# Moving 64 output columns of a second matmul from row-wise tiles of 512 to a transposed, full-array tile of 128

## The chip, the cores and the metric

The kernel runs on one core of a Trainium2 chip. The metric is device time in microseconds (us). The profile's "span", from the first to the last instruction of the program, is about 1.8 us shorter than the time that is quoted.

Two ways of reading matmul records are used below. The profile's lines give the busy time of groups of instructions. Where a line is not fine enough I use the *step*: the time from the start of one matmul record to the start of the next on TensorE. Matmuls overlap in the pipeline (a 512-column one is recorded as 379 ns, but one starts every 216 ns), so it is the steps, not the durations, that add up to the span. Steps are computed from start times in the traces.

## The reference

```python
# x: [1, 2048, 576], w1: [576, 4608], w2: [4608, 576], all bf16
h = x @ w1 + b1
h = relu(h) ** 2
out = h @ w2 + b2          # [1, 2048, 576]
```

## The kernel before

Rows are handled in four blocks of 512 (`SB`). The first matmul leaves `hT`, the hidden values transposed: 36 tiles (`NFT`) of 128 hidden features x 512 rows per block. Its contraction length, 576, is four and a half times 128. For 32 of the 36 tiles all of it is done in nine steps of 64 with *row tiles*: pairs of matmuls on 64 of the array's rows each, which run side by side. For the other four tiles (of three blocks; the first block does it in smaller pieces) four steps of 128 use the full array, and only the remaining half a step is a row tile.

The second matmul has 576 output columns and two forms. The first 512 are computed row-wise: 128 rows of `hT` are the stationary operand, 512 columns of `w2` stream past. The last 64 are computed transposed: 64 columns of `w2` are stationary, 512 rows of `hT` stream. As 64 columns fill half of the array, two blocks are done side by side as two column tiles, each with its own half of the partitions of PSUM, the memory that matmuls write to. That needs both blocks' `hT`, so the phase comes once per two blocks, and its result is transposed back by a DMA.

In the cuts below, `keep` holds an instruction in program order; `...` marks what is left out.

```python
SB = 512; DM = 512; DT = D - DM          # DT = 64
EDGES = [0, 384, 512]                    # the last tile alone is cut in two

def phase_t(sb):                         # blocks sb and sb + 1 together
    pt = ps_o.tile([P, SB], FP32, name="pt", tag="po")
    for i, ft in enumerate(t_order):
        for h in range(2):
            keep(nc.tensor.matmul(pt[h * DT:(h + 1) * DT, :], lhsT=w2_sb[:, ft, DM:D], rhs=hTs[sb + h][:, ft, :],
                                  start=(i == 0), stop=(i == NFT - 1)))
    # ... + bias on ScalarE, DMA transpose, one output DMA per block

def phase_b(sb, hT, last=False, dups=()):
    for jj in range(RT):                 # 4 tiles of 128 rows
        # ...
        edges = EDGES if last and jj == RT - 1 else [0, DM]
        for d0, d1 in zip(edges, edges[1:]):
            po = ps_o.tile([P, 512], FP32, name="po", tag="po")
            for i, ft in enumerate(ft_order):
                keep(nc.tensor.matmul(po[:, 0:d1 - d0], lhsT=hT[:, ft, jj * P:(jj + 1) * P],
                                      rhs=w2_sb[:, ft, d0:d1], start=(i == 0), stop=(i == NFT - 1)))
            # ... + bias on VectorE into o_sb, output DMA on the sync queue

# order on TensorE, once for blocks 0 and 1, once for blocks 2 and 3 (the two "halves"):
a_rows(1); a_full(1, "rows_first")       # row tiles, then full array
phase_t(0)                               # column tiles
phase_b(0, hTs[0], dups=(2, 3)); phase_b(1, hTs[1])     # full array
```

Of the kernel before, what the change touches and what calls it, by code (L numbers as in the profile page):

```python
# [17 lines left out]
def kernel(  # L18
# [9 lines left out]
    nc = tc.nc  # L28
    keep = tc.keep_in_program_order
    P = 128  # L30
    H = 64
    x2 = x.flatten_outer_dims()
    out2 = out.flatten_outer_dims()
    S, D = x2.shape
    F = w1.shape[1]
    NFT = F // P
# [6 lines left out]
    assert D == 576 and S % 512 == 0 and F % (2 * P) == 0  # L43
    SB = 512
    RT = SB // P
    DM = 512
    DT = D - DM

    const = ctx.enter_context(tc.tile_pool(name="const", bufs=1))
    wpool = ctx.enter_context(tc.tile_pool(name="wpool", bufs=1))  # L50
# [46 lines left out]
    nc.gpsimd.memset(b1_rows[:], 0.0)  # L97
    nc.gpsimd.dma_start(out=b1_rows[0:NFT, :], in_=b1.rearrange("(ft p) -> ft p", p=P))
    b2_col = const.tile([P, 1], BF16, name="b2_col")
    for h in range(2):  # L100
        nc.gpsimd.dma_start(out=b2_col[h * DT:(h + 1) * DT, :], in_=b2[DM:D].rearrange("(d o) -> d o", o=1))
    b2T = const.tile([P, 1], FP32, name="b2T")
    nc.gpsimd.tensor_copy(out=b2T[:], in_=b2_col[:])
    warm = const.tile([P, 1], FP32, name="warm")
# [25 lines left out]
    w2_sb = wpool.tile([P, NFT, D], BF16, name="w2_sb")  # L130
# [39 lines left out]
    hTs = {}  # L170
# [92 lines left out]
        ft_order += [G + j, G + NJ + j]  # L263

    t_order = ft_order[G:] + ft_order[:G]
    EDGES = [0, 384, 512]

    def phase_t(sb):
        pt = ps_o.tile([P, SB], FP32, name="pt", tag="po")
        for i, ft in enumerate(t_order):  # L270
            for h in range(2):
                keep(nc.tensor.matmul(pt[h * DT:(h + 1) * DT, :], lhsT=w2_sb[:, ft, DM:D], rhs=hTs[sb + h][:, ft, :],  # L272
                                      start=(i == 0), stop=(i == NFT - 1)))
        oT = tpool.tile([P, SB], BF16, name="oT", tag="oT")
        keep(nc.scalar.activation(out=oT[:], in_=pt[:], func=ACT.Identity, bias=b2T[:], scale=1.0))  # L275
        ot = tpool.tile([P, RT, P], BF16, name="ot", tag="ot")
        keep(nc.sync.dma_start_transpose(out=ot[:, :, :], in_=oT[:, :]))
        for h in range(2):
            r0 = (sb + h) * SB
            dst = out2[r0:r0 + SB, DM:D].rearrange("(j p) d -> p j d", p=P)  # L280
            keep(nc.sync.dma_start(out=dst, in_=ot[:, :, h * DT:(h + 1) * DT]))

    def phase_b(sb, hT, last=False, dups=()):
        for jj in range(RT):
            if jj < len(dups):
                dup_windows(dups[jj])
            rt = sb * RT + jj
            o_sb = opool.tile([P, DM], BF16, name="o_sb", tag="o_sb")
# [6 lines that stand above are left out]
                keep(nc.vector.tensor_tensor(out=o_sb[:, d0:d1], in0=po[:, 0:d1 - d0], in1=b2_bc[:, d0:d1], op=ALU.add))  # L295
                keep(nc.sync.dma_start(out=out2[rt * P:(rt + 1) * P, d0:d1], in_=o_sb[:, d0:d1]))
# [20 lines left out]
    load_xT(3)  # L317
    a_rows(1)
    a_full(1, "rows_first")
    phase_t(0)  # L320
    phase_b(0, hTs[0], dups=(2, 3))
    phase_b(1, hTs[1])
    alloc_hT(2)
# [2 lines left out]
    alloc_hT(3)  # L326
    a_rows(3)
    a_full(3, "rows_first")
    phase_t(2)
    phase_b(2, hTs[2])  # L330
    phase_b(3, hTs[3], last=True)

# [29 lines left out]
```

## Time and profile before

| | before |
|---|---|
| time, median of 3 runs (lowest to highest) | 291.75 us (291.16 to 291.76) |
| span of the profiled run | 289.8 us |
| TensorE busy | 98% |
| second matmul, row-wise (L293) | 123.8 us busy |
| second matmul, transposed (L272) | 15.9 us busy |

These are lines of the profile page of the kernel before: busy time and share of the span per engine, the clock per fortieth of the span, and the chain of work that ended last.

```profile
span 289.8 us, 4679 instructions
PE 285.1 (98%) x2017; PEld 133.7 (46%) x2032; DVE 79.5 (27%) x176; ACT 95.2 (33%) x152; POOL 2.8 (1%) x11
PEclk9999999999999999999999999999999999999999
PE 98%; issue 0%; DVE 0%
```

TensorE (PE) is busy 98% of the time and is 98% of the chain; no other engine is over 33% (PEld is TensorE's own weight loads, which overlap its matmuls). A change here is worth what it changes on TensorE.

### The profile page before, as it was taken

Reading aid. Unit: us, or ns where it says so; the run is one execution under the profiler, and the core shown is the slowest. Engines: PE = TensorE matmul, PEld = TensorE weight load, DVE = VectorE, ACT = ScalarE, POOL = GpSimd, SP = SyncE. Lnnn points to the kernel's source line nnn. Section 1 sums busy time; section 2 is a strip of 40 time slices with the busy share of each in tenths; the row PEclk is TensorE's granted clock in tenths of the full one; section 3 lists DMA queues with packets and bytes.
Section 4 is the critical chain, followed back from the end, with each engine's and each line's share of the span. In section 5 each row is a group of like instructions: output and inputs, shape, how many; then the busy total and the mean of one; then the engine's idle time right before and its main releaser. Section 6 shows DMA issues by size and latency. Waiting matters only on the chain.

```text
span 289.8 us, 4679 instructions
## 1 busy us (share of the span) xinstructions
PE 285.1 (98%) x2017; PEld 133.7 (46%) x2032; DVE 79.5 (27%) x176; ACT 95.2 (33%) x152; POOL 2.8 (1%) x11
## 2 busy tenths in 40 slices
PE   8999999999999999999999999999999999999996
PEld 5544444444444444444444444444445444444454
DVE  1644554444502100000025444444440000000001
ACT  2666666666500000000027666666670000000000
POOL 3000000000000000000000000000000000000000
PEclk9999999999999999999999999999999999999999
DMA  7999999400001000000000000000000200000000
GB/s 198 213 235 185 315 388 234 83 0 2 0 19 33 5 20 18 18 18 20 18 18 2 1 2 0 2 0 2 0 2 0 38 18 18 18 20 18 20 18 20
DMA packets 30581, 16.26 MB, mean 56 GB/s; under 512 B 14676, under 2 KB 30560, under 8 KB 30560
## 3 DMA queue, kind: packets, MB, share of 16 engines
q1 hardware_dynamic: 30176, 15.65, 21.7%
q8 instruction: 16, 0.26, 0.4%
q10 hardware_dynamic: 288, 0.30, 0.4%
q14 instruction: 5, 0.04, 0.0%
q0 software_dynamic: 96, 0.01, 0.0%
HBM read 11.36 MB, written 2.36 MB: 47 GB/s over the span
## 4 chain that ended last, share of the span: by engine, by line
PE 98%; issue 0%; DVE 0%
PE po L293 43%; PE ph L189 42%; PE pt L272 5%; PE pn L210 4%; PE pn L228 1%; PE wps L63 1%; PE tb L150 1%; PE ph L191 1%; PE pn L204 1%; DVE o_sb L295 0%; PE b1T_ps L167 0%; PE pn L206 0%
## 5 line engine op out<-in xcount | busy, mean ns | idle before, releaser
L191 PE MATMUL ph<-xTw,w_h 64*128 64x512 bf16 x576 | 124.6, 376 | 0.0
L189 PE MATMUL ph<-xTw,w_h 64*128 64x512 bf16 x576 | 124.6, 376 | 0.0
L293 PE MATMUL po<-w_sb,hT 128*128 128x512 bf16 (+2 forms) x600 | 123.8, 366 | 0.8 <-issue 0.3
L177 ACT ACTIVATE r<-ph,b1T 128x512 bf16<-128x512 f32 x128 | 81.0, 684 | 41.7 <-PE ph L191 41.7
L293 PEld LDWEIGHTS <-hT 128*128 128x128 bf16 x612 | 58.3, 98 | 66.7 <-issue 0.8
L189 PEld LDWEIGHTS <-w_h 64*128 64x128 bf16 x576 | 54.1, 94 | 68.3
L178 DVE TENSOR_TENSOR hT<-r 128x512 bf16<-128x512 bf16 x144 | 61.1, 425 | 75.9 <-ACT r L177 75.4
L191 PEld LDWEIGHTS <-w_h 64*128 64x128 bf16 x576 | 54.1, 94 | 0.0
L295 DVE TENSOR_TENSOR o_sb<-po,b_bc 128x512 bf16<-128x512 f32 (+2 forms) x17 | 11.2, 660 | 125.0 <-PE po L293 125.0
L177 ACT ACTIVATE r<-pn,b1T 128x512 bf16<-128x512 f32 x16 | 10.3, 687 | 68.7 <-PE pn L206 67.4
L272 PE MATMUL pt<-hT,w_sb 128*64 128x512 bf16 x144 | 15.9, 380 | 0.0
L272 PEld LDWEIGHTS <-w_sb 128*64 128x64 bf16 x144 | 8.0, 110 | 7.8 <-issue 0.8
L210 PE MATMUL pn<-xTw,w1n 128*128 128x512 bf16 x45 | 10.4, 379 | 0.4 <-issue 0.3
L210 PEld LDWEIGHTS <-w1n 128*128 128x128 bf16 x48 | 4.5, 98 | 6.0 <-issue 0.8
L275 ACT ACTIVATE oT<-pt,b2T 128x512 bf16<-128x512 f32 x2 | 1.4, 687 | 14.5 <-PE pt L272 14.5
L228 PE MATMUL pn<-xTw,w1n 128*128 128x256 bf16 x32 | 4.8, 304 | 0.0
L228 PEld LDWEIGHTS <-w1n 128*128 128x128 bf16 x32 | 3.4, 110 | 0.6
L63 PE MATMUL wps<-const-bfloat16-1.0 128*128 128x512 bf16 (+1 forms) x7 | 2.8, 581 | 0.8 <-PEq L346 0.8
L157 DVE COPY xTw<-tb 128x256 bf16<-128x256 bf16 x4 | 1.1, 292 | 6.6 <-PE tb L150 6.6
L120 DVE COPY xTw<-xTw 64x2048 bf16<-64x2048 bf16 x4 | 2.8, 690 | 0.2
L121 DVE COPY xTw<-xTw 64x2048 bf16<-64x2048 bf16 x4 | 2.7, 687 | 0.1
L159 ACT COPY xTw<-tb 128x256 bf16<-128x256 bf16 x4 | 1.3, 375 | 3.7 <-PE tb L150 3.7
(23 smaller groups left out, 16.9 us busy)
## 6 DMA issues: line engine op xcount, KB each, us to landing
w_sb<-in_w_dram SPq DMA_DIRECT2D x6, 864.0 KB, 9.6
w_h<-in_w_dram SPq DMA_DIRECT2D x14, 288.0 KB, 6.8
out_dram<-o_sb SPq DMA_DIRECT2D x15, 128.0 KB, 1.7
w_h<-in_w_dram SPq DMA_DIRECT2D x4, 144.0 KB, 3.6
w1n<-in_w_dram SPq DMA_DIRECT2D x4, 128.0 KB, 3.7
x_sb<-in_x_dram ACTq DMA_DIRECT2D x2, 144.0 KB, 2.8
x_sb<-in_x_dram SPq DMA_DIRECT2D x2, 144.0 KB, 3.3
out_dram<-ot SPq DMA_DIRECT2D x4, 64.0 KB, 1.8
```

The lines of the kernel that those rows point to most:

```text
L63: keep(nc.tensor.matmul(wps[:, 0:n], lhsT=ones[:, 0:P], rhs=ones[:, 0:n], start=True, stop=True))
L150: keep(nc.tensor.transpose(bank[:, slot, qc], xs[:, j, c0:c0 + P], ident[:]))
L177: keep(nc.scalar.activation(out=r[:], in_=bank[:], func=ACT.Relu, bias=b1T[:, ft:ft + 1], scale=1.0))
L178: keep(nc.vector.tensor_tensor(out=hTs[sb][:, ft, :], in0=r[:], in1=r[:], op=ALU.mult))
L189: keep(nc.tensor.matmul(bx[:], lhsT=w1_h[0:H, LO_C[i], jc], rhs=xT[0:H, LO_W[i], :], start=(i == 0), stop=(i == NC - 1)))
L191: keep(nc.tensor.matmul(by[:], lhsT=w1_h[H:P, UP_C[i], jc], rhs=xT[H:P, UP_W[i], :], start=(i == 0), stop=(i == NC - 1)))
L204: keep(nc.tensor.matmul(banks[2 * i][:], lhsT=w1n8[0:H, i, :], rhs=xT[0:H, SPC, :], start=start, stop=stop, skip_group_check=order == "k_o ...
L210: keep(nc.tensor.matmul(banks[g][:], lhsT=w1n[:, k, g * P:(g + 1) * P], rhs=xT[:, O + k, :], start=start, stop=stop))
L228: keep(nc.tensor.matmul(banks[g][:, hc], lhsT=w1n[:, k, g * P:(g + 1) * P], rhs=xT[:, O + k, hc], start=(h == 0 and k == 0), stop=False, s ...
L272: keep(nc.tensor.matmul(pt[h * DT:(h + 1) * DT, :], lhsT=w2_sb[:, ft, DM:D], rhs=hTs[sb + h][:, ft, :], start=(i == 0), stop=(i == NFT - 1)))
L293: keep(nc.tensor.matmul(po[:, 0:d1 - d0], lhsT=hT[:, ft, jj * P:(jj + 1) * P], rhs=w2_sb[:, ft, d0:d1], start=(i == 0), stop=(i == NFT - 1)))
L295: keep(nc.vector.tensor_tensor(out=o_sb[:, d0:d1], in0=po[:, 0:d1 - d0], in1=b2_bc[:, d0:d1], op=ALU.add))
```

## The change

The transposed part takes 128 columns instead of 64. Then it fills the array by itself, needs no column tiles and no second block, and runs once per block. The row-wise part shrinks from 512 to 448 columns.

```diff
-    DM = 512
-    DT = D - DM
+    DT = P
+    DM = D - DT
 ...
-    for h in range(2):
-        nc.gpsimd.dma_start(out=b2_col[h * DT:(h + 1) * DT, :], in_=b2[DM:D].rearrange("(d o) -> d o", o=1))
+    nc.gpsimd.dma_start(out=b2_col[:], in_=b2[DM:D].rearrange("(d o) -> d o", o=1))
 ...
-    EDGES = [0, 384, 512]
+    EDGES = [0, 320, DM]
 
-    def phase_t(sb):
+    def phase_t(sb, hT):
         pt = ps_o.tile([P, SB], FP32, name="pt", tag="po")
         for i, ft in enumerate(t_order):
-            for h in range(2):
-                keep(nc.tensor.matmul(pt[h * DT:(h + 1) * DT, :], lhsT=w2_sb[:, ft, DM:D], rhs=hTs[sb + h][:, ft, :],
-                                      start=(i == 0), stop=(i == NFT - 1)))
+            keep(nc.tensor.matmul(pt[:], lhsT=w2_sb[:, ft, DM:D], rhs=hT[:, ft, :],
+                                  start=(i == 0), stop=(i == NFT - 1)))
 ...                                     # one output DMA per call instead of two
-    phase_t(0)
+    phase_t(0, hTs[0])
+    phase_t(1, hTs[1])
 ...
-    phase_t(2)
+    phase_t(2, hTs[2])
+    phase_t(3, hTs[3])
```

More of the change, by code (lines that the diff above doesn't have):

```diff
@@ L277, in phase_t @@
         keep(nc.sync.dma_start_transpose(out=ot[:, :, :], in_=oT[:, :]))
-        for h in range(2):
-            r0 = (sb + h) * SB
-            dst = out2[r0:r0 + SB, DM:D].rearrange("(j p) d -> p j d", p=P)
-            keep(nc.sync.dma_start(out=dst, in_=ot[:, :, h * DT:(h + 1) * DT]))
+        dst = out2[sb * SB:(sb + 1) * SB, DM:D].rearrange("(j p) d -> p j d", p=P)
+        keep(nc.sync.dma_start(out=dst, in_=ot[:, :, :]))
     def phase_b(sb, hT, last=False, dups=()):
```

## The prediction

> **What bounds the kernel now.** TensorE, almost alone. The page's busy line gives PE 285.1 of 289.8 us (98%), DVE 27%, ACT 33%; the chain of waits is 98% PE, "issue" 0%; the granted clock is 1.000. Matmuls overlap in the pipeline, so I cost them by start-to-start steps between consecutive PE records. At 512 columns a full-array matmul starts every 216 ns; at 384 every 162.5 ns; at 128 every 56 ns. They lie on columns / 2.4 + about 2.6 ns, which is what the Trainium skill ("TensorE: Matmul & The Clock Gate", "Back-to-back issue gap") gives for the isolated gap, N/2.4 + 2.5. The weight loads (about 98 ns each in the groups by line) hide even under 56 ns steps. A pair of 64-column tiles (two matmuls 3 to 4 ns apart) also takes 216 ns per pair.
>
> **What is removed, added, moved.**
> Removed: 64 columns of each row-wise matmul. 540 of them go from 512 to 448 columns (estimate 448/2.4 + 2.6 = 189.3 ns): 540 x 26.7 ns = 14.4 us. The split last tile goes from 384 to 320: 36 x 26.7 = 1.0 us. Together -15.38 us.
> Added: the transposed part goes from 72 pairs of column tiles at 216 ns (15.55 us) to 144 full-array matmuls at 216 ns (31.1 us): +15.55 us. In columns streamed the two cancel exactly (576 x 64 = 72 x 512); what stays, +0.17 us, is the fixed 2.6 ns of 72 more slots.
> Also removed: the changes of array mode. The Trainium skill ("TensorEngine Tiling (Array Packing)", "Key Properties") says that a change of tiling mode drains the array. This trace agrees: entering the column-tile phase the step is 309 ns in place of 216 (+93), its first pair's step is 237 (+21), and leaving it the step is 537 (+321). That is 0.44 us for each of two phases, 0.87 us, and all of it goes, as the phase now has the mode of its neighbours. The row-tile changes (steps of 535 ns) stay.
> Off the path: two more ACT evictions of 0.69 us, two more output transposes, 448 in place of 512 columns on DVE (0.69 us each, every 7.8 us). Every po tile is drained long before its bank is needed again. The tail (last 128 columns, one 0.29 us eviction, one output DMA) stays as it is.
>
> **On the critical path:** all PE terms. 15.55 - 15.38 - 0.87 = -0.7 us, 0.25%.
>
> **Predicted time:** 291.0 us; 8 in 10 between 290.2 and 291.7. Faster by over 2%: 0.01; within 2%: 0.98; slower by over 2%: 0.01.
>
> **What would show it.** Row-wise matmuls of 128x448 at steps of 189 ns; transposed ones at 216 ns, 144 of them, both phases together 31.1 us against 16.4 us; no step above 220 ns on entering or leaving the transposed phases; row-wise output 109 us against 124; PE still 98% of the chain; granted clock still 1.000.
>
> **What would make it wrong.** 448-column steps longer than 189 ns (weight loads no longer hidden, or a floor); the drain remaining for another reason than the mode, which makes it +0.15 us slower in place of 0.7 faster; a lower clock from denser use of the array; a bank wait from two transposed accumulators in a row. Only steps of 200 ns or more at 448 columns would cost 2%.

## More of the kernel before

The groups by line and shape, of the kernel before; the columns are line, engine, operation, output<-inputs, array rows*columns, partitions x elements, count, then busy us and mean ns of one, then idle time before them.

```profile
L293 PE MATMUL po<-w_sb,hT 128*128 128x512 bf16 x528 | 115.9, 379 | 0.8 <-issue 0.3
L272 PE MATMUL pt<-hT,w_sb 128*64 128x512 bf16 x144 | 15.9, 380 | 0.0
L210 PE MATMUL pn<-xTw,w1n 128*128 128x512 bf16 x45 | 10.4, 379 | 0.4 <-issue 0.3
```

The 144 matmuls of L272 are 72 pairs; "128*64" is the column tile. On the profile page 2017 matmuls were recorded, but 2032 weight loads; each matmul has one weight load, so 15 matmul records are missing: L293 should have 540 of this shape and has 528, L210 should have 48 and has 45. The idle time "issue" in the last column belongs to those gaps.

The timeline of TensorE at the first transposed phase, kernel before (start us, length us, engine, line, operation, count, idle time before):

```profile
73.13 3.40 PE L210 MATMUL pn<-xTw,w1n 128*128 128x512 bf16 x15 [0.16 <-issue]
76.46 7.96 PE L272 MATMUL pt<-hT,w_sb 128*64 128x512 bf16 x72
84.58 1.67 PE L293 MATMUL po<-w_sb,hT 128*128 128x512 bf16 x7 [0.16 <-issue]
```

The phase of column tiles starts at 76.46 and the next one at 84.58 us, 8.12 us for 36 pairs, where 36 x 216 ns would be 7.78. The program has 16 matmuls of L210 here; 15 are in the trace. The matmul that is missing is the first one, which is why the line is marked with idle time.

Last, what the sync queue waited for at the end of the program (line 357 stands for the closing instructions; columns: in total us, times, longest):

```profile
SPq L357 <- DMA out_dram<-o_sb: 0.7, 1, 0.7
```

## The result and the profile after

| | before | changed |
|---|---|---|
| median (lowest to highest) | 291.47 us (291.16 to 291.76), 4 runs | 291.15 us (291.01 to 291.35), 4 runs |
| ratio, 95% interval | | 0.9992 (0.9978 to 1.0006) |
| five more rounds: median | 291.46 us, 9 runs | 291.18 us, 5 runs |
| ratio, 95% interval | | 0.9991 (0.9978 to 1.0003) |

A ratio and its interval are from runs of the same rounds; a ratio is not quite that of the medians (291.15 / 291.47 = 0.9989). Both intervals include 1: by the clock of whole runs the two kernels are the same.

The same lines of the changed kernel: page (with the chain last), groups, timeline, and the sync queue's wait.

```profile
span 289.4 us, 4699 instructions
PE 285.2 (99%) x2032; PEld 138.9 (48%) x2032; DVE 78.5 (27%) x176; ACT 96.7 (33%) x154; POOL 2.3 (1%) x10
PEclk9999999999999999999999999999999999999999
PE 97%; DMA 1%; SPq 0%; DVE 0%; issue 0%
```

```profile
L289 PE MATMUL po<-w_sb,hT 128*128 128x448 bf16 x540 | 102.5, 352 | 0.0
L270 PE MATMUL pt<-hT,w_sb 128*128 128x512 bf16 x144 | 31.4, 379 | 0.0
L209 PE MATMUL pn<-xTw,w1n 128*128 128x512 bf16 x48 | 10.9, 379 | 0.0
```

```profile
72.46 3.63 PE L209 MATMUL pn<-xTw,w1n 128*128 128x512 bf16 x16
75.92 15.70 PE L270 MATMUL pt<-hT,w_sb 128*128 128x512 bf16 x72
91.46 1.87 PE L289 MATMUL po<-w_sb,hT 128*128 128x448 bf16 x9
```

```profile
SPq L355 <- DMA out_dram<-o_sb: 1.1, 1, 1.1
```

This trace happens to be complete: 2032 matmuls, 2032 weight loads, and no "issue" in the idle column (the second profile of the same kernel has 2027). The row-wise tile takes steps of 189 to 190 ns, the transposed one 216, and both transposed phases start without a gap: 15.54 us for 72 matmuls. All of that is as predicted. The chain is 97% PE and not 98%, as the first microseconds of this run waited for a load of the first weight (the 1% DMA). The first row of L209 shows what an entry into another array mode costs when no record is missing: its step from the last row tile is 308 ns in place of 213, and its own is 227 in place of 216. In the kernel before, the same place reads as one step of 535 ns. 308 + 227 = 535: one record is missing, and the "long" step is two short ones.

The span can be cut exactly, because TensorE runs without a break from the first row tile to the last matmul. Times in us from the traces; "start-up" is the time of the first row-tile matmul, "second matmul" the stretches from the last row tile of a half to the first row tile of the next half, and to the last matmul of the kernel, "closing" from the start of the last matmul to the end of the span:

```
profiled run         start-up  first matmul  second matmul     closing  span
                               (both halves) half 1   half 2
before                 9.773   125.643       77.478   73.963   2.942    289.80
before, run again      9.626   125.676       77.478   73.963   2.933    289.68
changed                9.329   125.644       77.341   73.827   3.236    289.38
changed, run again     9.400   125.642       77.342   73.826   3.241    289.45
```

Everything but the start-up repeats to some hundredths of a microsecond. So differences that whole runs cannot resolve are plain here: the second matmul became 0.137 + 0.136 = 0.273 us shorter, and the closing 0.29 to 0.31 us *longer*. The two cancel: the span less the start-up is 280.03 and 280.05 us before, 280.05 and 280.05 us after. In the profiled runs all of the difference, 0.2 to 0.4 us, is then in the start-up, which is discussed below. That the same holds for the 0.3 us between the medians is likely but not shown, as most runs were not profiled.

Two things are to be explained: why the gain on TensorE is 0.27 us and not the 0.7 us of the prediction, and why the closing grew.

### The profile page after: what moved, and what is told of

Its sections match the earlier page's. It is cut to its first block, busy times and chain, and to the rows that moved or that the text cites. A ratio compares the mean times of both kernels' runs of the same rounds, so it can differ in the third digit from the quotient of the medians.

```text
span 289.4 us, 4699 instructions
## 1 busy us (share of the span) xinstructions
PE 285.2 (99%) x2032; PEld 138.9 (48%) x2032; DVE 78.5 (27%) x176; ACT 96.7 (33%) x154; POOL 2.3 (1%) x10
## 4 chain that ended last, share of the span: by engine, by line
PE 97%; DMA 1%; SPq 0%; DVE 0%; issue 0%
PE ph L188 42%; PE po L289 38%; PE pt L270 11%; PE pn L209 4%; DMA w1n<-in_w_dram 1%; PE pn L227 1%; PE ph L190 1%; PE pn L203 1%; SPq L75 0%; SPq L72 0%; DVE o_sb L291 0%; PE tb L149 0%; PE b1T_ps L166 0%; PE pn L205 0%
## 5 line engine op out<-in xcount | busy, mean ns | idle before, releaser
L289 PE MATMUL po<-w_sb,hT 128*128 128x448 bf16 (+2 forms) x612 | 109.4, 341 | 0.0
L291 DVE TENSOR_TENSOR o_sb<-po,b_bc 128x448 bf16<-128x448 f32 (+2 forms) x17 | 10.2, 597 | 125.8 <-PE po L289 125.8
L270 PE MATMUL pt<-hT,w_sb 128*128 128x512 bf16 x144 | 31.4, 379 | 0.0
L270 PEld LDWEIGHTS <-w_sb 128*128 128x128 bf16 x144 | 14.1, 98 | 17.0
L273 ACT ACTIVATE oT<-pt,b2T 128x512 bf16<-128x512 f32 x4 | 2.7, 687 | 28.3 <-PE pt L270 28.3
L209 PE MATMUL pn<-xTw,w1n 128*128 128x512 bf16 x48 | 10.9, 379 | 0.0
L209 PEld LDWEIGHTS <-w1n 128*128 128x128 bf16 x48 | 4.5, 98 | 6.0 <-issue 0.8
L227 PE MATMUL pn<-xTw,w1n 128*128 128x256 bf16 x32 | 4.2, 273 | 0.4 <-DMA w1n<-in_w_dram 0.2
L203 PE MATMUL pn<-xTw,w1n 64*128 64x512 bf16 x8 | 2.4, 379 | 0.0
```

Source lines behind the costliest of these rows:

```text
L203: keep(nc.tensor.matmul(banks[2 * i][:], lhsT=w1n8[0:H, i, :], rhs=xT[0:H, SPC, :], start=start, stop=stop, skip_group_check=order == "k_o ...
L209: keep(nc.tensor.matmul(banks[g][:], lhsT=w1n[:, k, g * P:(g + 1) * P], rhs=xT[:, O + k, :], start=start, stop=stop))
L227: keep(nc.tensor.matmul(banks[g][:, hc], lhsT=w1n[:, k, g * P:(g + 1) * P], rhs=xT[:, O + k, hc], start=(h == 0 and k == 0), stop=False, s ...
L270: keep(nc.tensor.matmul(pt[:], lhsT=w2_sb[:, ft, DM:D], rhs=hT[:, ft, :], start=(i == 0), stop=(i == NFT - 1)))
L291: keep(nc.vector.tensor_tensor(out=o_sb[:, d0:d1], in0=po[:, 0:d1 - d0], in1=b2_bc[:, d0:d1], op=ALU.add))
```

## The experiments

**Theories about TensorE.** *A*: a stay in the column-tile mode costs about 0.22 us in all for going in and out; 0.17 us for 72 more slots less 0.44 us for two stays gives -0.27 us. *B*, the step of the prediction: a stay costs 0.44 us, and -0.7 us results. *D*: it is not the mode but the alternation of operands, banks or phases.

### Both kernels again (r_before, r_after)

No edit.

> The kernel before, unchanged, profiled anew and timed against itself. In the first trace the steps around the column-tile phases were read as 309 ns (in), 237 ns (its first pair) and 537 ns (out). Theory A: the 537 ns is two steps of about 309 and 228 ns with one matmul record missing between them (216 ns of ordinary work), so a phase costs about 0.22 us in array-mode changes, not 0.44; a complete record here would show a step of about 308 ns out and then one of about 227 ns, and no step over 320 ns where the record is complete. Rival B (the step of the prediction): the change out of the mode really takes 321 ns more; the step of 537 ns stays even with a complete record (36 of 36 matmuls of that tile). Both: ratio 1.000 within 0.1%.

> The changed kernel, unchanged, timed over more rounds. Theory A: +0.17 us for 72 more PE slots, -0.44 us for the array-mode changes gone, so -0.27 us, ratio 0.9991. Rival B (the prediction): -0.7 us, ratio 0.9976. From the start of the last full-array matmuls ahead of the first transposed phase to the end of that half's row-wise output, 0.14 us shorter than before by A, 0.35 us by B.

Measured: the kernel before against itself 0.9996 (0.9982 to 1.0009), 291.27 us median; the changed one 0.9991 (0.9978 to 1.0003), which is A's number and leaves B's 0.9976 just outside. That is luck and no test of the two: the closing adds 0.3 us (0.0010) by either theory, so that a whole run should give 1.0001 by A and 0.9986 by B, and both lie inside the interval. The trace of the kernel before had the same gaps again (steps of 537 and 538 ns out of the two phases, with 282 of 288 matmuls recorded in the first half's row-wise output), so it did not settle how the long step is to be read. The gaps are regular, which is why a second profile repeats them: after the long step, every 50th row-wise matmul is without a record, seen as a step of 432 ns, twice 216, in either profile. The stretches did: 77.478 to 77.342 and 73.963 to 73.826 us, 0.136 and 0.137 us per half, as A has it.

### Each part alone (e1_added_only, e2_removed_only)

```diff
 # e1: row-wise part stays at 512 columns; transposed part as in the changed kernel, half of it thrown away
+    D0 = D - P
-            for h in range(2):
-                keep(nc.tensor.matmul(pt[h * DT:(h + 1) * DT, :], lhsT=w2_sb[:, ft, DM:D], rhs=hTs[sb + h][:, ft, :], ...
+            keep(nc.tensor.matmul(pt[:], lhsT=w2_sb[:, ft, D0:D], rhs=hT[:, ft, :], ...
+        keep(nc.sync.dma_start(out=dst, in_=ot[:, :, P - DT:P]))
 # e2: column tiles stay; row-wise part cut to 448, columns 448 to 511 not written
+    RW = D - P
-            edges = EDGES if last and jj == RT - 1 else [0, DM]
+            edges = EDGES if last and jj == RT - 1 else [0, RW]     # EDGES = [0, 320, RW]
```

> Only what the change adds: the last 128 columns full-array and transposed per block (64 of them are thrown away), row-wise part left at 512 columns. Correct result. Theory A: 72 pairs of 216 ns become 144 matmuls of 216 ns, +15.55 us, less 0.44 us of mode changes: +15.1 us, ratio 1.052. Rival B: +15.55 - 0.87 = +14.7 us, ratio 1.050. A rival in which full-array matmuls of 128 columns of weights cost more than a pair of half-width ones would show steps over 216 ns.

> Only what the change removes: row-wise part cut to 448 columns, the column-tile phases left as they were; columns 448 to 511 of the output are not written, so the result is wrong on purpose. All theories: 540 x 26.7 + 36 x 26.7 ns = -15.4 us, ratio 0.947; steps of 189 ns. If weight loads bound the shorter matmuls, steps stay over 195 ns and the gain is under 12 us.

Measured: e1 was correct and took 306.63 us, ratio 1.0523 (1.0508 to 1.0537); e2 was wrong and took 276.01 us, ratio 0.9473 (0.9458 to 0.9488). In the traces, the two stretches of the second matmul grew in e1 by 7.542 + 7.543 = 15.085 us and shrank in e2 by 7.681 + 7.680 = 15.36 us. Their sum, -0.276 us, is the effect of the whole change on TensorE (-0.273), so the parts simply add. Against 15.54 us for 72 more slots of 216 ns, e1's 15.085 leaves 0.455 us for the two stays in the mode: 0.23 us each. The weight loads bound nothing in e2: its 448-column groups are those of the changed kernel.

```profile
L294 PE MATMUL po<-w_sb,hT 128*128 128x448 bf16 x540 | 102.5, 353 | 0.0
```

### More stays in the mode (e3_weave6, e4_weave1)

The same work as before, with the column-tile pairs cut into chunks that stand between the full-array matmuls of the first row-wise tile of each half.

```diff
-    phase_t(0)
-    phase_b(0, hTs[0], dups=(2, 3))
+    phase_b(0, hTs[0], dups=(2, 3), weave=True)      # the same for blocks 2 and 3
 # in phase_b, after each matmul i of tile jj == 0:
+    if pt is not None and i % CH == CH // 2:         # CH = 6 in e3, 1 in e4
+        t_pairs(pt, sb, i // CH * CH, i // CH * CH + CH)
```

> The kernel before, with each column-tile phase cut into 6 chunks of 6 pairs that stand between the full-array matmuls of the first row-wise tile of its half: 12 stays in the column-tile mode in place of 2, all work the same. Theory A (0.22 us for going in and out): 10 x 0.22 = +2.2 us, ratio 1.0075. Rival B (0.44 us): +4.4 us, ratio 1.015. Rival D (what the phase's edges cost is not the mode but the switch between operands, banks or phases once): under +0.3 us.

> The same with 36 chunks of one pair: 72 stays in the mode in place of 2. Theory A: 70 x 0.22 = +15.3 us, ratio 1.053; step sizes of about 309 and 237 or, for single pairs, the same sum per stay. Rival B: 70 x 0.44 = +30.5 us, ratio 1.105. Rival D: under +1 us. If the cost of a stay is less for single pairs, because the drains of in and out overlap, between +8 and +15 us.

Measured: e3 293.60 us, ratio 1.0076 (1.0059 to 1.0093); e4 307.30 us, ratio 1.0546 (1.0531 to 1.0562). Both were correct. In the traces the stretches grew by 1.137 + 1.136 us in e3, 0.227 us for each of ten more stays, and by 7.953 + 7.954 us in e4, 0.227 us for each of seventy. A holds to the second digit, at two loads that differ seven times; B would have been twice that, and D is out as a cost that is paid once.

The timeline of TensorE in e3 shows both readings of the long step side by side:

```profile
76.90 1.49 PE L276 MATMUL pt<-hT,w_sb 128*64 128x512 bf16 x12
78.32 1.47 PE L300 MATMUL po<-w_sb,hT 128*128 128x512 bf16 x6
79.72 1.49 PE L276 MATMUL pt<-hT,w_sb 128*64 128x512 bf16 x12
81.37 1.24 PE L300 MATMUL po<-w_sb,hT 128*128 128x512 bf16 x5 [0.16 <-issue]
82.54 1.49 PE L276 MATMUL pt<-hT,w_sb 128*64 128x512 bf16 x12
```

Each chunk has six full-array matmuls in the program. Where six are recorded, the chunk starts 1.42 us after the start of the six pairs before it (78.32 - 76.90), without idle time. Where five are recorded, it seems to start 1.65 us after (81.37 - 79.72), with 0.16 us of "issue" before it. But the distance between the starts of two column-tile chunks is 2.82 us in both cases (79.72 - 76.90 and 82.54 - 79.72). Nothing stalled; the first matmul of that chunk left no record. The steps say the same: where the record is complete, 311 or 312 and then 225 to 227 ns; where it is not, one of 537 to 539 and then an ordinary 216. This is how the 537 ns of the prediction came about.

For e4 the same view shows a stay of a single pair:

```profile
76.99 0.41 PE L276 MATMUL pt<-hT,w_sb 128*64 128x512 bf16 x2
77.33 0.39 PE L300 MATMUL po<-w_sb,hT 128*128 128x512 bf16 x1
77.65 0.41 PE L276 MATMUL pt<-hT,w_sb 128*64 128x512 bf16 x2
```

One round of a pair and a full-array matmul takes 0.66 us (77.65 - 76.99) where two ordinary steps take 0.43.

### The same weave without the mode (e5_weave1_full)

```diff
 # the changed kernel; transposed matmuls one by one between the row-wise ones of tiles 0 and 1
-    phase_t(0, hTs[0]); phase_t(1, hTs[1])
+    # in phase_b, after matmul i of tile jj < 2:
+    t_one(pt, hTs[sb + jj], i)
```

> Control: the changed kernel with its full-array transposed matmuls woven one by one between the row-wise matmuls of the first two tiles of each half, so operands, banks and roles alternate at every matmul but the array mode never changes. Theory A and B (it is the mode): ratio to before as the changed kernel's, 0.999, steps alternating between 216 and 189 ns, no other. Rival D (alternation itself costs): up to 144 x 0.2 = +29 us.

Measured: correct, 291.36 us, ratio 0.9999 (0.9984 to 1.0014). The stretches, 77.341 and 73.826 us, are those of the changed kernel to a nanosecond or two. The timeline alternates at steps of 0.19 and 0.22 us (with steps of 405 ns, the sum of the two, where a record is missing; 2025 of 2032 are there):

```profile
75.89 0.35 PE L294 MATMUL po<-w_sb,hT 128*128 128x448 bf16 x1
76.08 0.38 PE L272 MATMUL pt<-hT,w_sb 128*128 128x512 bf16 x1
76.30 0.35 PE L294 MATMUL po<-w_sb,hT 128*128 128x448 bf16 x1
```

Operands, banks and roles change at every matmul here, at no cost. So it is the tile mode that cost 0.227 us per stay in e4, and D falls entirely.

### More slots for the same columns (e6_two_slots)

```diff
+    cuts = [d0, (d0 + d1) // 2, d1] if d1 - d0 == DM else [d0, d1]
+    for c0, c1 in zip(cuts, cuts[1:]):      # two matmuls of 224 columns instead of one of 448
```

> The changed kernel with each 448-column row-wise matmul issued as two of 224 columns, the same columns streamed in twice the slots (540 more). Theory: each slot carries a fixed 2.6 ns besides its columns, so +1.4 us against the changed kernel, ratio to before 1.004; steps of about 96 ns. This is the term that keeps +0.17 us for 72 more slots. If it is not per slot, ratio 0.999. If weight loads of 98 ns bind at this size, steps over 98 ns, so +3 us or more.

Measured: correct, 292.85 us, ratio 1.0046 (1.0031 to 1.0061). The stretches are 0.720 + 0.629 = 1.349 us longer than in the changed kernel, 2.50 ns for each of 540 more slots. 72 x 2.5 ns = 0.18 us is the price of the change's additional slots; 0.18 - 0.455 = -0.275 us is the whole of what TensorE gained. The steps are 95 to 96 ns, a little under the 98 ns that one weight load is recorded to take, although every one of these matmuls has a weight load of its own.

```profile
L291 PEld LDWEIGHTS <-hT 128*128 128x128 bf16 x1152 | 109.1, 98 | 1.8
```

The unaltered widths agree: in the first profile of the changed kernel the mean steps are 55.86, 135.86, 189.17 and 215.85 ns at 128, 320, 448 and 512 columns, each 2.5 ns over columns / 2.4.

**Theories about the closing.** The last output lands 2.03 to 2.04 us after the start of the last matmul in both kernels, and 2.02 to 2.04 us in all others. Then the sync queue takes its closing waits in a fixed order, one after the other, about 62 ns each. In the records the transfers issued by the sync and scalar queues take eight semaphores in turn. The kernel before has 64 such transfers, so the last output has the eighth semaphore, which is waited for last: all other waits are done while the output is still under way. The changed kernel has two more transposing transfers, 66 in all; its last output has the second semaphore, which is in the first of the closing waits, and the other five are still to be done after the landing. *T*: this order is the cause. *U*: the transposed outputs or the shape of the last writes are. *V*: it is the number of transfers. Experiments e1, e5 and e6 already had 66 transfers and a closing of 3.23 to 3.24 us; e2, e3 and e4 had 64 and 2.93 to 2.94 us. As e1 writes the same last tile as the kernel before, and e2 that of the changed one, the shape of the last writes is out already.

### Other numbers of transfers (e7_before_plus2, e8_after_minus2, e9_after_plus4)

Only the loads of the second weight are cut differently; the last of them lands at 46.6 to 47.9 us, and the second matmul starts at about 76 us.

```diff
-    for c in (0, 3, 1, 4, 2, 5):
-        load_w2(c)                              # 6 loads of 6 tiles
+    # e7, on the kernel before: the last two loads cut in two     -> 66 transfers
+    # e8, on the changed kernel: (0,6) (18,24) (6,18) (24,36)     -> 64 transfers
+    # e9, on the changed kernel: the last four loads cut in two   -> 70 transfers
```

> About the tail, found in the traces: from the start of the last matmul to the end of the span it is 3.02 us in the changed kernel and 2.72 us before, although the last output lands at the same 2.03 us in both. Theory T: the closing waits on the sync queue are taken in a fixed order, one step of about 62 ns each; the transfers of the sync and scalar queues take eight semaphores in turn, and the changed kernel, with two more of them (66 for 64), ends on the semaphore that is waited for first, so five steps are left to do after the landing, while before ended on the one waited for last. This run: the kernel before with two of its loads of the second weight cut in two (66 transfers, nothing else). T: last matmul to end 3.02 us, +0.30 us; PE work unchanged (77.478 and 74.182 us for the two second-matmul stretches). Rival U (it is the transposed outputs or the shape of the last writes): 2.72 us, unchanged.

> The changed kernel with four loads of the second weight in place of six, so 64 transfers as before. T: last matmul to end 2.72 us, 0.30 us less than the changed kernel, so this one has both gains, -0.27 us of PE time against the kernel before and no longer tail: ratio to before 0.9990 less whatever start-up gives, too small for the clock of rounds, but to be read in the trace. U: 3.02 us.

> The changed kernel with ten loads of the second weight in place of six (70 transfers): the last output takes the sixth semaphore of the eight, after which two waits are left. T: last matmul to end about 2.84 us (between 2.78 and 2.90), shorter than in the changed kernel although there are more transfers. A rival in which each further transfer lengthens the tail (V): over 3.02 us. U: 3.02 us.

In these texts "last matmul to end" is counted from the modelled end of the last matmul, 0.219 us after its start, except for the 2.03 us of the landing, which counts from the start (the words "from the start" in the first of them fit only that number). Its 74.182 us for the second stretch is also counted to the modelled end: 73.963 + 0.219. Measured, all three correct:

```
                    ratio to before         second matmul      transfers  last      last matmul's  modelled end
                    (95% interval)          half 1   half 2               semaphore start to end   to end (expected by T)
e7_before_plus2     1.0010 (0.9998-1.0023)  77.477   73.963    66         2nd       3.302          3.083 (3.02)
e8_after_minus2     0.9989 (0.9976-1.0001)  77.340   73.826    64         8th       2.950          2.731 (2.72)
e9_after_plus4      0.9994 (0.9980-1.0007)  77.341   73.827    70         6th       3.059          2.840 (2.84)
```

What the sync queue waited for at the end, in e7, e8 and e9:

```profile
SPq L366 <- DMA out_dram<-o_sb: 1.1, 1, 1.1
```

```profile
SPq L360 <- DMA out_dram<-o_sb: 0.8, 1, 0.8
```

```profile
SPq L366 <- DMA out_dram<-o_sb: 0.9, 1, 0.9
```

The wait that the last output ends is 1.1 us long when it is the first of the closing waits, because it begins early; 0.7 to 0.8 us when it is the last, as the other waits have been done meanwhile. A longer single wait here means more waits *behind* it. T holds in all three: the tail of the kernel before can be made long (e7), that of the changed kernel short (e8), and with four transfers more it is shorter than with none more (e9), which rules out V. e7 came out 0.06 us over the expectation, one more step: the kernel before makes seven closing waits, as its third GpSimd transfer, the second small bias load, has a semaphore of its own; the changed kernel makes six.

e8 has both gains. Without the start-up its span is 289.187 - 9.428 = 279.76 us, against 280.03 and 280.05 for the kernel before and 280.05 for the changed one. It is 0.27 to 0.29 us better than the former and 0.29 us better than the latter. Its median was 290.91 us; by the clock of whole runs that is not separable from the kernel before (0.9976 to 1.0001), and it was not timed against the changed kernel in the same rounds.

**The start-up** stays open as far as this goes: over 13 profiled runs it was between 9.17 and 10.09 us, 9.17, 9.30, 9.49, 9.63, 9.77 and 10.09 with the two small bias loads of the kernel before, and 9.30, 9.33, 9.35, 9.40, 9.43, 9.50 and 9.68 with the one of the changed kernel. The groups overlap throughout. One difference is visible in the records: in the first profile before, the transposes at the beginning still took steps of 107 ns, in the first profile after already 56 ns. It does not explain the scatter: the shortest start-up of all, 9.17 us in e7, has steps of 107 ns too, and in the first profile after the chain spends 3.9 us on a load of the first weight. These runs do not show that the change had a part in it.

## Why the prediction was right or wrong

The time was right: 291.0 us was predicted, 290.2 to 291.7, and 291.15 was measured, within 2% as the chances had it. Part of the way there was not, and the closeness of the number is luck: it started from 291.75 us, the median of three runs, where four gave 291.47 and nine others 291.46, so that 0.7 us less would have been 290.8; a base too high and a gain too large made up for each other. The range also contained the kernel before.

- *TensorE bounds the kernel, and the columns cancel.* Right. -15.38 us predicted for the shorter row-wise part, -15.36 measured (e2). +15.55 predicted for the transposed part; 15.085 + 0.455 = 15.54 measured (e1 with the mode's part added back). Steps of 189 and 216 ns as predicted.
- *"+0.17 us ... the fixed 2.6 ns of 72 more slots."* Right: 2.50 ns per slot in e6, so 0.18 us.
- *"That is 0.44 us for each of two phases, 0.87 us."* Here a term of the sum was mis-sized; that the changes of mode cost time and disappear was right (e3, e4, e5). Going in and out costs 0.227 us, two phases 0.455 us. The step of 537 ns out of the mode was two steps, 312 and 226 ns, with one matmul record missing between them (shown in e3); 216 ns of ordinary work was booked as a stall. The sum becomes 0.18 - 0.455 = -0.275 us, and -0.273 was measured. The warning was on the page: 2017 matmuls against 2032 weight loads.
- *"The tail ... stays as it is."* Wrong. Eviction and last output are as before, and the output lands at the same moment, but the closing grew by 0.29 to 0.31 us, since two additional transfers shifted the last output from the last to the first of the closing waits (e7, e8, e9). This took back what TensorE had gained.
- *Off the path: evictions, transposing transfers, PSUM banks.* Right: no new wait of TensorE, and the three groups of the changed kernel shown above have no idle time.
- *-0.7 us in all.* Not confirmed. Between start-up and end, the change gave nothing: -0.273 us on TensorE, about +0.30 us in the closing, and 280.03 and 280.05 us against 280.05 and 280.05 us in all. What the profiled runs gained is in a start-up that scatters by 0.9 us, and in either series the interval of the ratio includes no change at all. A range of 1.5 us could not have told -0.7 from 0; the cut of the span did.

## What to carry to other kernels

Before a piece of work is moved from one tile shape to another, count the columns that stream on TensorE in both: here 576 x 64 equals 72 x 512, so the answer was close to nothing from the outset, and only the fixed costs (2.5 ns per slot, 0.227 us per stay in a column-tile mode) could tell the two apart. Compare the count of matmul records with that of weight loads before a long step is called a stall: a step that is one ordinary step too long is likely a missing record. In a kernel where everything else repeats to a hundredth of a microsecond, cut the span into start-up, work and closing, and look at which transfer the closing waits end on; the number of transfers can decide it.

## What the Trainium skill lacked or had wrong

- "TensorEngine Tiling (Array Packing)", section "Key Properties", says that a change of tiling mode drains the array, which the delays in these traces agree with, but gives no figure: in and out of a column-tile mode cost 0.227 us together (e3, e4), while a change of operands, banks and roles within one mode cost nothing (e5).
- "TensorE: Matmul & The Clock Gate", section "Back-to-back issue gap", gives N/2.4 + 2.5 ns for an isolated matmul, and for streams of weight load and matmul pairs a sustained 131 ns at 512 columns and 81 ns at 128. Here the first form holds for the stream itself, each matmul with its own weight load: 216 ns at 512, 189 at 448, 96 at 224, 56 at 128. The sustained figures of this section do not fit at either end.
- The same page, section "LDWEIGHTS (loading the stationary operand)", gives P/1.2 ns, from which one estimates 107 ns for 128 columns and 53 ns for 64. Recorded were 98 ns for 128 columns once the kernel was under way, which did not hold matmuls back even at steps of 56 and 96 ns, and 110 ns for the 64-column loads of the column tiles (L272 of the kernel before; two at a time).
- No page that was consulted tells how matmul records that are missing from a profile are recognised: 2017 of 2032 in the first profile before, a false step of 537 ns as the result.
- No page that was consulted tells how long a program's closing waits on its transfers take, or in which order: about 62 ns each and in a fixed order, so that the closing took 2.95 to 3.24 us in the changed kernel, depending on which semaphore the last output had (e8, e9 and the changed kernel itself).
